# Two attention and mixer layers on one core: VectorE's exponentials in 16-bit fixed point, merged key norms, wider odd units, weights on another queue, and a new order

## The chip, the core and the metric

One core of a Trainium2 chip runs the whole program. Its engines work side by side and meet only through semaphores: TensorE (PE, matmuls from SBUF into PSUM; its weight loads are listed apart as PEld), VectorE (DVE, elementwise work and reductions), ScalarE (ACT, activation functions from tables), GpSimd (POOL) and SyncE (SP, which issues most of the DMAs). PSUM has eight banks of 128x512 fp32 values. The metric is the device time of one execution in microseconds.

## The reference

x is 2048 tokens of 448 values. Two layers, each an attention block and a mixer block with the same weights in both layers:

```python
def _A_ref(x, wqkv, wo):                 # 16 heads of 28
    qkv = (x @ wqkv).reshape(B, S, 3, H, Dh).transpose(2, 0, 3, 1, 4)
    scores = einsum("bhqd,bhkd->bhqk", q, k) * (Dh ** -0.5)
    p = softmax(scores)
    o = einsum("bhqk,bhkd->bhqd", p, v)
    return o.transpose(0, 2, 1, 3).reshape(B, S, D) @ wo
def _B_ref(x, w1, w2, w3, w4):
    h = gelu(layernorm(x) @ w1)
    hs = concat(quarters of h shifted by 1, -1, 2, -2 tokens) @ w2
    x1 = x + hs
    return x1 + gelu(layernorm(x1) @ w3) @ w4
x = x + _A_ref(layernorm(x), A_wqkv, A_wo)
x = x + _B_ref(layernorm(x), B_w1, B_w2, B_w3, B_w4)
# and both once more
```

Most of the elementwise work is the softmax: 2 layers x 16 heads x 2048 x 2048 exponentials, that is 2048 blocks of 128 keys by 512 queries.

## The kernel before

**A planner writes the program.** Every task is a Python generator (t_scores, t_exp, t_pv, k_proj, t_mixA and so on) that yields operations with an estimated duration, waits for named events, and acquires and releases buffers and PSUM banks. A list scheduler (class Sched) plays them through on a model of the engines and writes down, for each engine, the order in which the operations are issued; semaphores follow from reads and writes. Priorities (RANK), leads (Q_LEAD), shares (R_RATE, D_RATE), thresholds and choices of engine (XPAR) are tables of numbers at the top of the file. So a change of a number or of one estimated duration moves the order everywhere. Where the model sees TensorE idle, it inserts filler matmuls (filler, L2165); idle_share is the filler's share of a window, which decisions use.

**Attention.** The work is cut into 68 segments: a layer, a chunk of queries, a group g of four heads, a range of keys. For each segment, blocks of 128x512 scores are computed by TensorE into PSUM banks (L1416). t_scores collects them into units: even units use banks 0, 1, 2 and odd units banks 3, 4. t_exp takes the exponential of a whole unit with one ScalarE instruction (L1654) into the ring PT of 15 slots, and t_pv multiplies by the values into a bank of its own, bank 5 (L825). Queries and keys carry extra rows so that the exponent is shifted by a bound made from key norms; vaug holds the values with a column of ones, which gives the sum.

**VectorE's blocks.** Some blocks are taken out of the stream ahead of time, either in place of the third block of an even unit (R_RATE, bank 2) or as an additional block in a miscellaneous bank (D_RATE, bank 6 or 7), and VectorE computes their exponential. d_first (L1498) writes y = scores x constant as a 32-bit fixed-point number with 16 bits of fraction, and d_chain does the rest: two SCALAR_TENSOR_TENSORs in fp32 evaluate a polynomial in the fraction (L1525, L1527), a TENSOR_SCALAR finishes it into bf16 (L1529), and a last one adds the integer part to the exponent bits (L1532). The estimated durations are in DST. A block is only taken if a buffer for y and a result slot are free, if the planner's recent VectorE load is below XPAR['dt'] (R) or idle_share is at least XPAR['ft'] (D), and as the rates allow.

**Key norms.** For each chunk of keys and each group of heads, k_proj projects (L834), copies the keys out (L1182), squares them (L1168, on GpSimd or VectorE), sums the squares per head with a matmul against astat, and takes the maximum over the keys on VectorE (L1195). t_bias and t_bias4 make the shift from it, which the query projections wait for.

**Other elementwise work.** After each chunk's attention come the output projection and the mixer (t_outproj, t_mixA, t_mixB, t_w4). Their gelu is either a tanh form on ScalarE under the exponential's table, with VectorE and GpSimd doing the rest (tanh_gelu, L1932 to L1935), or a real gelu in a session of its own, with a table load before and after (L2118; L1916 for a chunk that has joined a session).

**Start.** SP issues four tiles of x, then the weights for keys and queries as four DMAs (L860, L862), then wv and the rest of x. ScalarE fills the pads of vaug (L946, L948), packs the weights (t_pack, L963) and squares the first chunks (L975), from which t_ratio makes a scale. t_ln1_first normalises four tiles, TensorE transposes them (L1059), and the first projections follow.

```python
yield op("dve", c_ps(512), lambda e: e.tensor_scalar(out=y, in0=ps[:, bi(bank), :], scalar1=SCALE * L2E * FS, scalar2=-126.0 * FS, op0=ALU.mult, op1=ALU.max),
yield op(D_[0][0], D_[0][1], lambda e: e.scalar_tensor_tensor(out=q, in0=lo, scalar=E2 / E3 * FS, in1=lo, op0=ALU.add, op1=ALU.mult),
```

Of the kernel before, what the change touches and what calls it, by code (L numbers as in the profile page):

```python
# [7 lines left out]
ALU = mybir.AluOpType  # L8
# [176 lines left out]
class Sched:  # L185
# [140 lines left out]
    def keep_pe_busy(self, until):  # L326
# [8 lines left out]
        while True:  # L335
# [21 lines left out]
            if pick is None:  # L357
                if not fits:
                    break
                if self.open5 and all(d.t_end + 0.2 <= t for d in self.P.deps("pe", reads, [key("b5")]).values()):  # L360
                    f_ = self.P.add("pe", lambda e: fn(e, "b5"), reads + [(("xn", 0), "pad")], [key("b5")], t_end=t + dur)
# [188 lines left out]
DST = [('dve', 0.6), ('dve', 0.6), ('dve', 0.34), ('dve', 0.6)]  # L550
DSEG = 1
R_RATE = {(0,): 0, (1,): 0.17, (2,): 0.183, (3,): 0.152, (4,): 0, (5,): 0, (6,): 0.274, (7,): 0.096, (8,): 0.106, (9,): 0.193, (10,): 0.073, (11,): 0.196, (12,): 0.228, (13,): 0, (14,): 0, (15,): 0.457, (16,): 0.306, (17,): 0, (18,): 0, (19,): 0.082, (20,): 0, (21,): 0.089, (22,): 0, (23,): 0.481, (24,): 0, (25,): 0.086, (26,): 0.053, (27,): 0.007, (28,): 0.051, (29,): 0.263, (30,): 0.207, (31,): 0.244, (32,): 0, (33,): 0.012}
# [3 lines left out]
DWIN = 3.0  # L556
# [5 lines left out]
RANK = {('q', 0, 1): 1, ('q', 0, 2): 1.763, ('q', 0, 3): 1.176, ('q', 1, 0): 1.162, ('q', 1, 1): 1.21, ('q', 1, 2): 1.085, ('q', 1, 3): 1.967, ('b', 0, 0): 3, ('b', 0, 1): 2.77, ('b', 0, 2): 1.853, ('b', 0, 3): 2.798, ('b', 0, 4): 1.211, ('b', 1, 0): 2.781, ('b', 1, 1): 1.849, ('b', 1, 2): 2.32, ('b', 1, 3): 2.579, ('b', 1, 4): 2.042, ('a', 0, 0): 1.98, ('a', 0, 1): 1.742, ('a', 0, 2): 1.882, ('a', 0, 3): 1.528, ('a', 0, 4): 2.263, ('a', 1, 0): 2.618, ('a', 1, 1): 1.108, ('a', 1, 2): 1.44, ('a', 1, 3): 1.223, ('a', 1, 4): 1.214, ('k', 0, 1): 2.594, ('k', 0, 2): 2.273, ('k', 0, 3): 2.136, ('k', 1, 0): 2.166, ('k', 1, 1): 1.68, ('k', 1, 2): 1.231, ('k', 1, 3): 2.338, ('k', 1, 4): 2.507, ('c', 0, 0): 1.464, ('c', 0, 1): 1, ('c', 0, 2): 2.866, ('c', 0, 3): 2.39, ('c', 0, 4): 1.764, ('c', 1, 0): 1.835, ('c', 1, 1): 1.44, ('c', 1, 2): 2.171, ('c', 1, 3): 2.127, ('c', 1, 4): 2.53, ('w', 0, 0): 2.816, ('w', 0, 1): 1.099, ('w', 0, 2): 2.277, ('w', 0, 3): 2.222, ('w', 0, 4): 1.537, ('w', 1, 0): 1.87, ('w', 1, 1): 2.531, ('w', 1, 2): 2.03, ('w', 1, 3): 2.877, ('w', 1, 4): 3, ('o', 0, 0): 2.728, ('o', 0, 1): 1.549, ('o', 0, 2): 1.72, ('o', 0, 3): 1.329, ('o', 0, 4): 2.769, ('o', 1, 0): 2.974, ('o', 1, 1): 3, ('o', 1, 2): 1.615, ('o', 1, 3): 1.476, ('o', 1, 4): 1.611, ('v', 0, 1): 1.389, ('v', 0, 2): 2.811, ('v', 0, 3): 3, ('v', 1, 0): 2.33, ('v', 1, 1): 1.844, ('v', 1, 2): 1, ('v', 1, 3): 1.537, ('v', 1, 4): 2.768, ('l', 1, 0): 1.014, ('l', 1, 1): 1.661, ('l', 1, 2): 2.714, ('l', 1, 3): 2.867, ('l', 1, 4): 1.565}  # L562
Q_LEAD = {(0, 1): 14, (0, 2): 51, (0, 3): 92, (1, 0): 95, (1, 1): 20, (1, 2): 92, (1, 3): 88}
D_RATE = {(0,): 0.062, (1,): 0.096, (2,): 0.608, (3,): 0.377, (4,): 0, (5,): 0, (6,): 0.055, (7,): 0.125, (8,): 0.318, (9,): 0.311, (10,): 0.716, (11,): 0.411, (12,): 0, (13,): 0.489, (14,): 0.575, (15,): 0.471, (16,): 0, (17,): 0.052, (18,): 0.128, (19,): 0, (20,): 0.201, (21,): 0.579, (22,): 0.043, (23,): 0.016, (24,): 0.849, (25,): 0.568, (26,): 0.41, (27,): 0.05, (28,): 0.449, (29,): 0, (30,): 0.392, (31,): 0.346, (32,): 0.42, (33,): 0.104}
PE_NORM = {(0, 0): False, (0, 1): False, (0, 2): False, (0, 3): False, (0, 4): False, (0, 5): False, (0, 6): True, (0, 7): True, (1, 0): False, (1, 1): False, (1, 2): False, (1, 3): False, (1, 4): True, (1, 5): True, (1, 6): False, (1, 7): True}
# [9 lines left out]
XPAR = {'l0': 6, 'l1': 11, 'l2': 15, 'x0': 14, ('mg', 0, 0): 0, ('mg', 0, 1): 0, ('mg', 0, 2): 0, ('mg', 0, 3): 1, ('mg', 0, 4): 0, ('mg', 1, 0): 0, ('mg', 1, 1): 1, ('mg', 1, 2): 0, ('mg', 1, 3): 0, ('mg', 1, 4): 1, 'rp': 0.167, 'dp': 3.141, 'dt': 0.642, 'ft': 0.011, ('tw', 0, 0): 0, ('tw', 0, 3): 0, ('tw', 0, 7): 0, ('tw', 0, 11): 1, ('tw', 0, 13): 0, ('tw', 1, 0): 0, ('tw', 1, 3): 0, ('tw', 1, 7): 0, ('tw', 1, 11): 0, ('tw', 1, 13): 0, ('ek', 0, 0): 2, ('eo', 0, 0): 2, ('ek', 0, 1): 0, ('eo', 0, 1): 1, ('ek', 0, 2): 2, ('eo', 0, 2): 2, ('ek', 0, 3): 0, ('eo', 0, 3): 2, ('ek', 0, 4): 0, ('eo', 0, 4): 2, ('eq', 0, 0): 1, ('eq', 0, 1): 1, ('eq', 0, 2): 0, ('eq', 0, 3): 0, ('ez', 0, 0): 2, ('ez', 0, 3): 0, ('ez', 0, 7): 1, ('ez', 0, 11): 2, ('ez', 0, 13): 0, ('ez', 0, 4): 0, ('ez', 0, 8): 0, ('ez', 0, 12): 1, ('ez', 0, 14): 1, ('ex', 0, 0): 2, ('ex', 0, 1): 0, ('ex', 0, 2): 2, ('ex', 0, 3): 2, ('ex', 0, 4): 2, ('ex', 0, 5): 0, ('ex', 0, 6): 2, ('ex', 0, 7): 1, ('ex', 0, 8): 2, ('ex', 0, 9): 1, ('ex', 0, 10): 2, ('ex', 0, 11): 2, ('ex', 0, 12): 0, ('ex', 0, 13): 1, ('ex', 0, 14): 0, ('ex', 0, 15): 2, ('ek', 1, 0): 0, ('eo', 1, 0): 2, ('ek', 1, 1): 1, ('eo', 1, 1): 2, ('ek', 1, 2): 0, ('eo', 1, 2): 1, ('ek', 1, 3): 0, ('eo', 1, 3): 1, ('ek', 1, 4): 1, ('eo', 1, 4): 0, ('eq', 1, 0): 0, ('eq', 1, 1): 0, ('eq', 1, 2): 0, ('eq', 1, 3): 1, ('ez', 1, 0): 1, ('ez', 1, 3): 1, ('ez', 1, 7): 2, ('ez', 1, 11): 2, ('ez', 1, 13): 0, ('ez', 1, 4): 2, ('ez', 1, 8): 2, ('ez', 1, 12): 2, ('ez', 1, 14): 1, ('ex', 1, 0): 2, ('ex', 1, 1): 0, ('ex', 1, 2): 2, ('ex', 1, 3): 0, ('ex', 1, 4): 2, ('ex', 1, 5): 2, ('ex', 1, 6): 1, ('ex', 1, 7): 0, ('ex', 1, 8): 0, ('ex', 1, 9): 0, ('ex', 1, 10): 0, ('ex', 1, 11): 2, ('ex', 1, 12): 0, ('ex', 1, 13): 1, ('ex', 1, 14): 0, ('ex', 1, 15): 0}  # L575
GMERGE = {}
WARM = 0.5
# [22 lines left out]
def build_kernel(nc, A_x, A_wqkv, A_wo, B_x, B_w1, B_w2, B_w3, B_w4, out, n_layers=2):  # L600
# [18 lines left out]
    FS = 65536.0  # L619
    GK = 0.044715  # L620
    E0, E1, E2, E3 = 0.99992525, 0.69583285, 0.22606939, 0.07802301
# [58 lines left out]
    with st:  # L680
# [103 lines left out]
        def op(eng, dur, fn, reads=(), writes=(), **kw):  # L784
            if eng == "pool":
# [1482 lines left out]
```

## Time and profile before

| what | us |
|---|---|
| median of 3 runs | 1028.11 (1027.86 to 1029.22) |
| profiled execution | 1027.56, its span 1025.8 |
| first exponential of the attention starts | 16.20 |
| last one ends | 972.70 |
| 128x1536 exponentials on ScalarE, mean of one | 1.552 (356 of them) |
| 128x1024 exponentials on ScalarE, mean of one | 1.124 (435 of them) |
| VectorE's first step (L1498), to yd / to vaug | 0.687 / 0.684 (85 / 25 of them) |
| gelu sessions' table loads on ScalarE | 1.283 each |

TensorE's granted clock is 1.000 over the span. The views used are: the page (busy time by engine, the chain that ended last); groups of instructions by line, engine and shape, with their count, busy time, the mean of one in ns, and the idle time before them with what ended it; busy time by stretches of the span; and the timeline, which lists an engine's instructions with start and duration. On VectorE and ScalarE the record of an instruction reaches past the start of the next one, so durations do not add up to busy time, and the distance between two starts says what an instruction takes of the engine.

### The profile page before, as it was taken

What the parts mean: (1) busy time and instruction counts of PE and PEld (TensorE: products, weight loads), DVE (VectorE), ACT (ScalarE), POOL (GpSimd) and SP (SyncE); (2) the same over time, 40 slices, a digit from 0 to 9 for tenths busy, and PEclk for the clock granted to TensorE, in tenths of its full rate; (3) what the DMA queues carried; (4) which work ended last, traced back from release to release, by engine and by line L of the source; (5) the groups of instructions that cost most, each with busy time, mean ns of one, the idle gap of its engine ahead of it and who ended that gap; (6) DMA issues with size and microseconds to landing.
All of it is one profiled execution on the core that took longest, in us unless ns stands there. A gap on an engine that the chain in (4) does not pass through costs nothing.

```text
span 1025.8 us, 35791 instructions
## 1 busy us (share of the span) xinstructions
PE 973.6 (95%) x16053; PEld 403.7 (39%) x16053; DVE 830.9 (81%) x1616; ACT 982.3 (96%) x903; POOL 255.0 (25%) x370
## 2 busy tenths in 40 slices
PE   8999999999999999999999999999999999899998
PEld 3333344333343334434334333333334333344465
DVE  7977899989869787878788778898999787787652
ACT  7999999999999999999999999999999999999942
POOL 2124132433134204342233111012313020231120
PEclk9999999999999999999999999999999999999999
DMA  4433453311104003231132015334212111121000
GB/s 121 118 90 103 126 166 89 60 33 38 24 26 98 18 14 100 54 54 24 27 91 77 12 62 161 102 73 120 59 29 38 23 47 41 33 64 36 13 21 24
DMA packets 98808, 64.38 MB, mean 63 GB/s; under 512 B 70816, under 2 KB 87536, under 8 KB 98656
## 3 DMA queue, kind: packets, MB, share of 16 engines
q1 hardware_dynamic: 95280, 54.02, 20.4%
q0 software_dynamic: 3376, 8.09, 2.9%
q8 instruction: 125, 2.05, 0.9%
q14 instruction: 27, 0.22, 0.1%
HBM read 28.16 MB, written 16.76 MB: 44 GB/s over the span
## 4 chain that ended last, share of the span: by engine, by line
ACT 73%; PE 23%; DVE 3%; DMA 0%; issue 0%; SPq 0%; DVEq 0%
ACT PT L1654 65%; PE ps L834 13%; PE ps L1416 5%; PE ps L825 4%; ACT h2T L2118 3%; ACT fb L1934 1%; ACT L1654 1%; PE ps L2165 1%; ACT L2118 1%; DMA PT<-in_A_wqkv_dram 0%; ACT sq L1165 0%; ACT vaug L2118 0%; DVE ub L1738 0%; ACT hT L1916 0%; DVE qT L1217 0%
## 5 line engine op out<-in xcount | busy, mean ns | idle before, releaser
L1654 ACT ACTIVATE PT<-ps 128x1024 bf16<-128x1024 f32 (+1 forms) x791 | 887.0, 1316 | 5.4 <-PE ps L1416 4.1
L1416 PE MATMUL ps<-qT,kT 32*128 32x512 bf16 (+1 forms) x2560 | 309.0, 340 | 27.6 <-ACT PT L1654 19.4
L825 PE MATMUL ps<-PT,vaug 128*32 128x512 bf16 (+1 forms) x2428 | 242.4, 341 | 0.1
L1416 PEld LDWEIGHTS ps<-qT,kT 32*128 32x128 bf16 x2560 | 79.3, 91 | 297.3 <-ACT PT L1654 271.1
L834 PE MATMUL ps<-xT,w 128*32 128x512 bf16 (+4 forms) x2592 | 178.6, 343 | 2.8 <-DVE hT L1903 1.5
L2165 PE MATMUL ps<-ident 128*32 128x256 bf16 x2648 | 121.4, 277 | 1.8 <-POOL ident L919 1.5
L825 PEld LDWEIGHTS ps<-PT,vaug 128*32 128x32 bf16 x2428 | 72.0, 95 | 85.8 <-issue 72.6
L834 PEld LDWEIGHTS ps<-xT,w 128*32 128x32 bf16 (+1 forms) x2592 | 69.9, 95 | 53.8 <-issue 24.6
L834 PE MATMUL ps<-w,h2T 128*32 128x448 bf16 x1288 | 86.2, 355 | 4.1 <-ACT h2T L2118 4.0
L2165 PEld LDWEIGHTS ps<-ident 128*32 128x32 bf16 x2648 | 76.3, 97 | 25.7 <-issue 9.9
L1498 DVE TENSOR_SCALAR yd<-ps 128x512 int32<-128x512 f32 x85 | 58.4, 687 | 20.2 <-PE ps L1416 19.1
L2094 DVE CAST h2T<-ps 128x384 bf16<-128x384 f32 (+1 forms) x84 | 51.9, 618 | 24.4 <-PE ps L834 23.7
L1763 POOL TENSOR_TENSOR otn<-ub,fb 128x512 bf16<-128x512 f32 (+1 forms) x24 | 29.4, 1227 | 127.1 <-DMA fb<-rscr 115.1
L1527 DVE SCALAR_TENSOR_TENSOR fb<-fb,yd 128x512 f32<-128x512 f32 x81 | 60.3, 748 | 0.6
L1525 DVE SCALAR_TENSOR_TENSOR fb<-yd 128x512 f32<-128x512 uint16 x81 | 59.6, 741 | 0.5
L1532 DVE SCALAR_TENSOR_TENSOR PD<-yd,PD 128x512 int16<-128x512 int16 x80 | 56.5, 709 | 1.0
L834 PEld LDWEIGHTS ps<-w,h2T 128*32 128x32 bf16 x1288 | 33.7, 96 | 33.2 <-issue 12.4
L1168 POOL TENSOR_TENSOR sq<-qT 128x512 bf16<-128x512 bf16 x20 | 24.4, 1221 | 85.3 <-DVE qT L1217 85.3
L1168 POOL TENSOR_TENSOR sq<-kT 128x512 bf16<-128x512 bf16 (+2 forms) x24 | 22.9, 955 | 90.6 <-DVE kT L1182 62.4
L834 PE MATMUL ps<-xT,wk_pad 128*32 128x512 bf16 (+1 forms) x512 | 42.8, 369 | 0.1
L834 PE MATMUL ps<-wo_pad,otn 128*32 128x448 bf16 x512 | 38.0, 355 | 2.0 <-DVE x_res L1818 1.6
L2007 POOL TENSOR_SCALAR mst<-mv 128x1 f32<-128x1 f32 x32 | 8.5, 268 | 123.7 <-DVE mv L1021 111.4
(210 smaller groups left out, 1319.7 us busy)
## 6 DMA issues: line engine op xcount, KB each, us to landing
uscr<-ub SPq DMA_DIRECT2D x28, 256.0 KB
ub<-uscr SPq DMA_DIRECT2D x28, 256.0 KB, 3.1
fb<-rscr SPq DMA_DIRECT2D x96, 64.0 KB, 2.0
xnd<-xn SPq DMA_DIRECT2D x28, 128.0 KB, 2.0
x_res<-in_A_x_dram POOLq DMA_DIRECT2D x16, 224.0 KB, 4.3
xd<-x_res SPq DMA_DIRECT2D x16, 224.0 KB, 2.2
x_res<-xd SPq DMA_DIRECT2D x16, 224.0 KB, 2.7
out_dram<-obf SPq DMA_DIRECT2D x16, 112.0 KB, 1.7
```

The costliest lines, as they stand in the source:

```text
L825: return lambda e: e.matmul(out=out, lhsT=lhsT, rhs=rhs, start=start, stop=stop, **kw)
L834: r.append(e.matmul(out=out[c:c + w, :], lhsT=lhsT[:, c:c + w], rhs=rhs, start=start, stop=stop, tile_position=(0, c)))
L1168: return both(kp, 0.15 + NW * 0.0018, 0.07 + NW * 0.00052, lambda e: e.tensor_tensor(out=sq[:, si, 0:NW], in0=src, in1=src, op=ALU.mult), ...
L1416: yield op("pe", (0.005 + NW * 0.00042) / nc_, lambda e, i=i, kc=kc, j=j, g=g, a=a, NW=NW, bank=bank: e.matmul(out=ps[:, bank, i * NW:(i + ...
L1498: yield op("dve", c_ps(512), lambda e: e.tensor_scalar(out=y, in0=ps[:, bi(bank), :], scalar1=SCALE * L2E * FS, scalar2=-126.0 * FS, op0=A ...
L1525: yield op(D_[0][0], D_[0][1], lambda e: e.scalar_tensor_tensor(out=q, in0=lo, scalar=E2 / E3 * FS, in1=lo, op0=ALU.add, op1=ALU.mult), re ...
L1527: yield op(D_[1][0], D_[1][1], lambda e: e.scalar_tensor_tensor(out=q, in0=q, scalar=E1 / E3 * FS * FS, in1=lo, op0=ALU.add, op1=ALU.mult) ...
L1532: yield op(D_[3][0], D_[3][1], lambda e: e.scalar_tensor_tensor(out=pdt.bitcast(I16), in0=hi, scalar=128.0, in1=pdt.bitcast(I16), op0=ALU. ...
L1654: yield op("act", 0.0635 + n * w * 0.000833, lambda e, bk=bk, s0=s0, n=n, w=w: e.activation(out=PT[:, s0:s0 + n, 0:w], in_=ps[:, bk[0]:bk[ ...
L2094: ev = op("dve", c_ps(m * NW), lambda e, hr=hr, pv=pv: e.tensor_copy(out=hr, in_=pv), reads=[("ps", bi(b))], writes=hk, touch=[b])
L2118: yield op("act", c_act(len(fr_) * NW), lambda e, v=v: e.activation(out=v, in_=v, func=ACT.Gelu_apprx_tanh), reads=allk, writes=allk, tab= ...
L2165: return [e.matmul(out=ps[32 * c:32 * c + 32, bi(b), 0:256].rearrange("p (a n) -> p a n", n=128), lhsT=xn[:, 0, D:D + 32] if live else ide ...
```

## The change

- **VectorE's exponential.** FS falls from 65536 to 256: d_first now writes y as int16 with 8 bits of fraction (into the first half of the same buffer). d_chain becomes seven operations on 16-bit data: shift and flip the sign to centre the fraction, a linear term, a square, a scaling, a product, an addition onto y, and a shift that turns the fixed-point number into the bits of a bf16. The result is twice the exponential, so ScalarE's exponentials get a bias of log 2.
- **Key norms.** Except for the first chunk, k_proj ends after the copy. A new task t_knorm squares the four groups of a chunk (into sq and obf buffers), sums them with four matmuls into the four quarters of one bank, and takes one maximum; two small operations and a small matmul distribute it. The bias tasks wait for it.
- **Units.** The PV accumulator moves from bank 5 to bank 7, bank 5 becomes a miscellaneous bank, and an odd unit may take it as third bank when idle_share(8.0) is at least XPAR['wt']. PT's slots are given out in turn (place), and t_exp waits for the blocks that used them before.
- **Start.** The weights for keys and queries are issued by ScalarE's queue as five DMAs (t_wload). Only the pads of vaug's first four slots are filled on ScalarE, the others on GpSimd after the start. Transposes of the first tiles are done tile by tile, and the packing order changes.
- **Order.** All tables of numbers are new; among them XPAR['ft'] from 0.011 to 0.14, XPAR['dt'] from 0.642 to 0.658, and the first layer's chunk 1 joins a gelu session (("mg", 0, 1) from 0 to 1). The sum of the rates times blocks goes from 262 to 217 for R_RATE and from 601 to 582 for D_RATE. Estimated transfer times of the later weights grow. st6 and the bias tables shrink.

```diff
-DST = [('dve', 0.6), ('dve', 0.6), ('dve', 0.34), ('dve', 0.6)]
+DST = [0.2, 0.2, 0.336, 0.2, 0.336, 0.336, 0.2]
...
+PVBANK = 7
...
-    FS = 65536.0
+    FS = 256.0
-    E0, E1, E2, E3 = 0.99992525, 0.69583285, 0.22606939, 0.07802301
+    EA, EB, EG = 21.0427, 88.0467, -0.244205
...
-        MISC = ["b6", "b7", "b5", "b4", "b3", "b2", "b1", "b0"]
+        MISC = ["b6", "b5", "b7", "b4", "b3", "b2", "b1", "b0"]
...
+        def t_wload():
+            for (ci, a, n, t) in ((1, 0, 3, 4.6), (1, 3, 1, 4.3), (0, 0, 1, 4.2), (0, 1, 2, 5.0), (0, 3, 1, 4.6)):
+                src = A_wqkv[128 * a:min(128 * (a + n), D), ci * D:(ci + 1) * D]
+                d3 = wsts[ci]
+                if a == 3:
+                    yield dma("act", lambda e, d3=d3, src=src: e.dma_start(out=d3[0:64, 3, :], in_=src), writes=[("pt", 4 * ci + 3)], t=t, iss=0.55)
...
-            yield op("pool", 0.15, lambda e: e.memset(dcol[:, 0:1], G2 * FS * FS), writes=[("dcol",)])
+            yield op("pool", 0.15, lambda e: e.memset(dcol[:, 0:1], math.log(2.0)), writes=[("dcol",)])
...
+        def t_knorm(L, c):
+            t0, n = KC[L][c]
+            NW = 128 * n
...
+            held = []
+            for g in range(4):
+                yield ("wait", ("k", L, g, c))
...
+                s = yield ("acq", ["ob0", "ob1"] + SQ, dk)
...
+                yield both(("ek", L, c), 0.15 + NW * 0.0018, 0.07 + NW * 0.00052, lambda e, buf=buf, src=src: e.tensor_tensor(out=buf, in0=src, in1=src, op=ALU.mult), dk, [key])
+            b = yield misc(*[h[2] for h in held])
+            yield op("pe", max(0.21, c_mm(NW)), lambda e: [e.matmul(out=ps[32 * g:32 * g + 32, bi(b), 0:NW], lhsT=ind8[:, :], rhs=held[g][1], start=True, stop=True, tile_position=(0, 32 * g)) for g in range(4)],
...
+            yield op("dve", c_ps(NW), lambda e: e.reduce_max(out=kmx[:, :], in_=ps[:, bi(b), 0:NW], axis=AX.X), reads=[("ps", bi(b))], writes=[("kmx",)], touch=[b])
...
+            yield ("sig", ("kn", L, c))
...
-            return (0, 1, 2)[:len(units[u])] if u % 2 == 0 else (3, 4)[:len(units[u])]
+            return (0, 1, 2)[:len(units[u])] if u % 2 == 0 else (3, 4, 5)[:len(units[u])]
...
+            yield op("dve", D_[0], lambda e: e.tensor_scalar(out=qu, in0=yu, scalar1=8, scalar2=32768, op0=ALU.logical_shift_left, op1=ALU.bitwise_xor),
+            yield op("dve", D_[1], lambda e: e.tensor_scalar(out=w, in0=qa, scalar1=EA / 65536.0, scalar2=EB, op0=ALU.mult, op1=ALU.add),
+            yield op("dve", D_[2], lambda e: e.tensor_tensor(out=z, in0=qa, in1=qa, op=ALU.mult),
+            yield op("dve", D_[3], lambda e: e.tensor_scalar(out=z, in0=z, scalar1=1.0 / 65536.0 ** 2, scalar2=EG, op0=ALU.mult, op1=ALU.add),
+            yield op("dve", D_[4], lambda e: e.tensor_tensor(out=z, in0=z, in1=w, op=ALU.mult),
+            yield op("dve", D_[5], lambda e: e.tensor_tensor(out=ya, in0=ya, in1=z, op=ALU.add),
+            yield op("dve", D_[6], lambda e: e.tensor_scalar(out=pdt.bitcast(U16), in0=yu, scalar1=32768, scalar2=1, op0=ALU.bitwise_xor, op1=ALU.logical_shift_right),
...
+                if u % 2 == 1 and SC.idle_share(8.0) >= XPAR['wt']:
+                    gw = yield ("try", [["b5"]])
+                    if gw is not None:
+                        widened.add(u)
+                        lim = 3
...
-                if u >= 6:
-                    for (si, kb, j) in units[u - 6]:
-                        yield ("wait", ("pv", si, kb))
+                for (si, kb) in before[u]:
+                    yield ("wait", ("pv", si, kb))
```

More of the change, by code (lines that the diff above doesn't have):

```diff
@@ L1337, in t_bias4 @@
             yield ("wait", ("rtn",))
[L1338 to L1340 removed]
+            for c in range(p):
+                yield ("wait", ("kn", L, c))
             src, sk = kmaxc[:, L, :, 0], [("kmaxc", L, g, 0) for g in range(4)]
```

216 lines of the change are left out of this document (141 added, 75 removed).

## The prediction

> **What bounds the kernel now.** I read the page's engine totals first, then the three stages, the chain of waits, ScalarE's and VectorE's groups by shape, and last the timeline where VectorE is full.
>
> ```profile
> PE 973.6 (95%) x16053; PEld 403.7 (39%) x16053; DVE 830.9 (81%) x1616; ACT 982.3 (96%) x903; POOL 255.0 (25%) x370
> ...
> ACT 73%; PE 23%; DVE 3%; DMA 0%; issue 0%; SPq 0%; DVEq 0%
> ```
>
> ```profile
> 0.00:16.20 16.20, 12.77 (x239) 7.33 (x243) 11.48 (x51) 11.43 (x17) 5.32 (x18) 1.00 0.67 190
> 16.20:972.70 956.50, 911.01 (x14666) 364.92 (x14666) 799.77 (x1527) 950.61 (x857) 241.73 (x336) 1.00 0.25 63
> 972.70:1025.80 53.10, 49.87 (x1158) 31.44 (x1152) 19.62 (x39) 20.22 (x31) 7.92 (x16) 1.00 0.07 22
> ```
>
> The columns of the second fence are the stretch, its length, then busy time of PE, weight loads, DVE, ACT, POOL. I cut at the first and after the last exponential of the attention. In between, ScalarE is busy 950.6 of 956.5 us: this stage is as long as ScalarE's work. The 16.2 us ahead of it are a chain over all engines, and the 53.1 us behind it belong to TensorE (49.9 busy).
>
> ```profile
> L1654 ACT ACTIVATE PT<-ps 128x1536 bf16<-128x1536 f32 x356 | 552.5, 1552 | 5.0 <-PE ps L1416 4.1
> L1654 ACT ACTIVATE PT<-ps 128x1024 bf16<-128x1024 f32 x435 | 476.0, 1124 | 0.5
> ...
> L1527 DVE SCALAR_TENSOR_TENSOR fb<-fb,yd 128x512 f32<-128x512 f32 x81 | 60.3, 748 | 0.6
> L1525 DVE SCALAR_TENSOR_TENSOR fb<-yd 128x512 f32<-128x512 uint16 x81 | 59.6, 741 | 0.5
> L1498 DVE TENSOR_SCALAR yd<-ps 128x512 int32<-128x512 f32 x85 | 58.4, 687 | 20.2 <-PE ps L1416 19.1
> L1532 DVE SCALAR_TENSOR_TENSOR PD<-yd,PD 128x512 int16<-128x512 int16 x80 | 56.5, 709 | 1.0
> L1529 DVE TENSOR_SCALAR PD<-fb 128x512 bf16<-128x512 f32 x86 | 38.2, 446 | 0.8
> ...
> L1195 DVE TENSOR_REDUCE kmaxc<-ps 128x1 f32<-128x512 f32 x24 | 16.4, 682 | 2.9 <-PE ps L834 2.8
> ...
> L1438 DVE TENSOR_SCALAR qT<-qT,db 128x512 bf16<-128x512 bf16 x28 | 8.3, 348 | 0.1
> ...
> L1168 DVE TENSOR_TENSOR sq<-qT 128x512 bf16<-128x512 bf16 x8 | 3.4, 422 | 0.1
> ```
>
> 356x3 + 435x2 = 1938 of the 2048 score blocks (128x512) go through ScalarE; the other 110 (85 of L1498 above and 25 written to spare vaug slots) go through VectorE. Records overlap, so I price by the distance from one start to the next in the timeline: 1.331 us for three banks, 0.904 for two, hence 0.427 a bank and 0.050 an instruction; a block costs ScalarE (356x1.331 + 435x0.904)/1938 = 0.447 us. The same 791 distances add up to 884 us against 867 at these prices, so a perfect order has about 17 us to find.
>
> ```profile
> 500.60 0.68 DVE L1527 SCALAR_TENSOR_TENSOR fb<-fb,yd 128x512 f32<-128x512 f32 x1
> 501.31 0.43 DVE L1529 TENSOR_SCALAR PD<-fb 128x512 bf16<-128x512 f32 x1
> 501.66 0.61 DVE L1818 TENSOR_TENSOR x_res<-x_res,ps 128x448 f32<-128x448 f32 x1
> ```
>
> L1529 needs L1527's result and starts 0.71 us after it; L1818 needs nothing of L1529 and starts 0.35 after it, before its 0.43 us record has ended. A dependent neighbour costs some 0.11 to 0.12 us more than an independent one; medians are 0.60 against 0.72 for L1525 and L1527.
>
> **VectorE's chain.** Before, per block: 0.608 (L1498) + 2x0.602 + 0.336 + 0.602 = 2.75 us with independent neighbours; the mean distances found are 0.62 + 0.67 + 0.70 + 0.41 + 0.62 = 3.02, so 0.27 goes to dependent neighbours and to waits for GpSimd. After, L1498 stays; four TENSOR_SCALARs and three TENSOR_TENSORs follow, all on 16-bit data in SBUF. For the first the nearest row is L1438, 0.263 start to start with its scalar read from memory; a scalar from memory costs 0.060 (L1217 at 0.668 against L1903 at 0.608, both from PSUM), so 0.203 with an immediate. For the second it is L1168, 0.338. Sum 0.608 + 4x0.203 + 3x0.338 = 2.43 us. The waits: at least the 0.27 of before (2.70, saving 0.32), at most 7/4 of it because seven instructions follow where four did (2.91, saving 0.11). I take 0.20, between the two, as in the full stretches two chains interleave: 110x0.20 = 22 us (12 to 35).
>
> The Trainium skill (VectorE: DVE Perf Modes, Rules for kernel authors) speaks against the change: the pipeline drains after every operation, so the count of operations is to be kept low. It gives about 150 cycles of fixed cost at 0.96 GHz; by that the chain would take an estimated 3.18 us before and 3.12 after. The distances above differ from it: a one-per-cycle operation follows an independent one after 0.60, not 0.69 us.
>
> **No row shows the integer forms** (shift, exclusive or, int16 into bf16). Bounds: 0.203 (L1438's form) and 0.602 (L1532, int16, another form). I take 0.203, the row of the same operation and element size.
>
> **Key norms.** Of 36 maxima (L1195), four of the first chunk stay and 32 become 8. Removed 20x0.60 + 8x0.474 + 4x0.34 = 17.2 us; added 4.3 for eight maxima and 16 small operations at 0.13 (bias rows of L1330 and L1332) = 2.1. VectorE gains 10.8 us, and TensorE 24 groups of four matmuls, some 6 us (16 such take 1.03 in the timeline). The squares stay. The bias operations now wait for all four groups of a chunk; the cover is that they are due segments before their queries, and ScalarE's list of waits names none of them after the first unit. Without it, a late chunk holds ScalarE for about a maximum and two small operations, 0.9 us, eight times at most.
>
> **A gelu joined.** The first layer's second chunk joins an existing gelu session: four tanh at 0.52 become one 1.82, nothing for ScalarE, but eight L1933/L1935 operations of 0.60 leave VectorE: 4.8 us.
>
> **What VectorE's time buys.** 22 + 10.8 + 4.8 = 38 us, at 2.82 a block, is 13 more blocks; 13x0.447 = 5.9 us off ScalarE. From the bounds: 28/2.91 = 10 to 51/2.70 = 19 blocks; none if the planner's new gates refuse them (a bank of TensorE's slack must now be 0.14 idle rather than 0.011, and the summed caps fall from 864 to 799). Low end 0, high end 8.5 us.
>
> **Three-bank odd units.** They need TensorE's filler at 0.166 of the last 8 us. Counting L2165's matmuls over the timeline, 91 of 395 odd units would meet it. Each widened unit carries three blocks and saves 0.4 of an instruction: 91x0.4x0.050 = 1.8 us; they take bank 5 from VectorE's blocks, so 1.0 (0 to 1.8).
>
> **Start.** Before, ScalarE's first packing (L963) starts at 6.63 us, behind two vaug fills of 3.27 us and a 1.24 us wait for weights that SP issued at 2.67. After: five issues on ScalarE's queue, priced by SP's for weights (0.43 to 0.60, so 2.6 us), a table load of 1.28 and a short fill of about 0.5 give 0.79 + 2.6 + 1.28 + 0.5 = 5.2 us. SP is rid of four issues (2.1 us), so wv and the next tiles of x come earlier. Transposes go tile by tile; before, five waited in TensorE's queue from about 8 to 9.27 us behind the sums of squares. VectorE's four statistics, up to 5.85 us, remain. I take 1.8 us off the 16.2 (0 to 2.4). The rest of the vaug pads moves to POOL, two memsets after the start; queued behind them are the key squares, and POOL idles 75%.
>
> **Order.** Priorities, leads and rates are new everywhere. The prize is at most the 17 us above; the loss is in the last 53 us, where TensorE is full and work put off lands at full price (five groups such as those between 1002.9 and 1023.0, 4 us each, are the scale, two of them a bad case: 8 us). I take 2 us of gain.
>
> **Sum.** Against the profiled execution's own 1027.56 us (span 1025.8; the median of the runs is 1028.11, 0.05% above): 1027.6 - 5.9 - 1.0 - 1.8 - 2.0 = 1016.9. **Forecast 1017 us.**
>
> **Rivals.** (1) *The short instructions save nothing* (waits grow with their number): only 15.6 us of VectorE are freed, at 3.02 five blocks, 2.3 us: 1020.5. For it, L1527 to L1529 at 0.71; against it, that two chains do interleave. 0.15. The page's rule cited above leads to this case.
>
> (2) *VectorE takes many more blocks.* Rates are now above zero in nearly every segment, and outside the full stretches named below VectorE is busy 648 of 796 us, 81%. Ten more points over some 700 us is 70/2.82 = 25 blocks, 11 us: 1006. Against it: TensorE is full there. 0.20.
>
> (3) *Slower: an integer form runs at one element a cycle.* In 160 us (116-176, 236-256, 656-696, 736-776) VectorE is busy 151.6, and holds 38 of the 110 blocks. One slow instruction adds 0.40 a block, 15 us there, which nothing hides: blocks land late, the PV matmuls wait, PT slots stay taken and ScalarE stops. The decision is at 10.7/38 = 0.28 us a block, so one slow instruction is enough (1032), and two give 1047. For it: L1532 at 0.602; against it: L1438. 0.08.
>
> (4) *The order gives it back*: banks held by widened units or a tail longer by 8 to 13 us, 1025 to 1030. For it: TensorE at 95%. 0.12.
>
> **How the numbers follow.** Forecast 0.45, rivals 0.15, 0.20, 0.08, 0.12. The forecast and the first two are faster (0.80); of the fourth, half is within 0.2%, about what a measurement can tell from no change here (1026 to 1030), and half is slower or, with the third, 0.14. The range runs from below rival 2's 1006 to the middle of rival 4, 1003 to 1029; the likeliest case alone spans 1010 to 1022.
>
> **What would show it.** The exponential chain's seven instructions behind the first at 0.29 and 0.42 us a record (right) or 0.69 (rival 3); about 123 blocks on VectorE against 110 (rival 2: 140 and more); maxima of keys 12 rather than 36; three-bank instructions on some 90 odd units; the first exponential near 14.4 us; the stage behind the last one still about 53 us. The forecast is wrong if ScalarE shows more than 15 us of waits in the middle stage.

## The result, and the profile after

| | median us (lowest to highest) | ratio to before, 95% interval |
|---|---|---|
| before | 1028.37 (1027.86 to 1029.22) | |
| after | 1093.88 (1091.77 to 1096.46) | 1.0637 [1.0611, 1.0663] |
| forecast | 1017 (1003 to 1029) | |

The change makes the kernel 6.4% slower. Where does the time sit? The page's busy times and its chain of waits for the kernel after:

```profile
PE 998.4 (91%) x16151; PEld 409.5 (37%) x16154; DVE 821.6 (75%) x2012; ACT 1044.3 (95%) x897; POOL 217.1 (20%) x349
...
ACT 89%; PE 8%; DVE 2%; issue 1%; DMA 0%; POOL 0%; SPq 0%; DVEq 0%
```

ScalarE's busy time went from 982.3 to 1044.3 us with six instructions fewer, while VectorE's fell. The three stages, cut as before at the first and after the last exponential (stretch, length, then busy time of PE, weight loads, DVE, ACT, POOL, then the granted clock):

```profile
0.00:18.01 18.01, 13.85 (x210) 7.63 (x211) 12.79 (x50) 8.69 (x16) 7.80 (x20) 0.81 0.59 170
18.01:1043.15 1025.14, 936.72 (x14842) 371.96 (x14843) 789.76 (x1924) 1015.63 (x853) 201.65 (x313) 1.00 0.23 59
1043.15:1094.50 51.35, 47.84 (x1100) 29.91 (x1100) 19.02 (x39) 19.97 (x30) 7.61 (x16) 0.99 0.07 23
```

Of the 68.7 us between the two spans, 68.6 lie in the middle stage, and ScalarE is still busy in all but 9.5 us of it. So it doesn't wait more: its own work has grown. The groups by shape say which:

```profile
L1754 ACT ACTIVATE PT<-ps,sc 128x1536 bf16<-128x1536 f32 x351 | 606.1, 1776 | 5.5 <-PE ps L1487 4.4 <-PE ps L831 1.0
L1754 ACT ACTIVATE PT<-ps,sc 128x1024 bf16<-128x1024 f32 x439 | 546.8, 1341 | 1.9 <-PE ps L1487 1.9
...
L1584 DVE TENSOR_SCALAR yd<-ps 128x512 int16<-128x512 f32 x84 | 57.7, 688 | 34.7 <-PE ps L1487 33.6
L1615 DVE TENSOR_TENSOR fb<-fb 128x512 bf16<-128x512 int16 x96 | 40.9, 431 | 0.6
L1621 DVE TENSOR_TENSOR yd<-yd,fb 128x512 int16<-128x512 int16 x76 | 31.9, 421 | 1.0
L1619 DVE TENSOR_TENSOR fb<-fb,yd 128x512 bf16<-128x512 bf16 x76 | 31.8, 421 | 0.9
L1617 DVE TENSOR_SCALAR fb<-fb 128x512 bf16<-128x512 bf16 x96 | 29.5, 312 | 0.7
```

The exponentials read one thing more: `ps,sc` stands where before had `ps`. sc holds dcol, the log 2 that the change adds as a bias, read from SBUF. A record of 128x1536 grew from 1552 to 1776 ns, one of 128x1024 from 1124 to 1341. By the distance between two starts it is 1.423 against 1.331 us and 0.996 against 0.904: **0.092 us more on each exponential, whatever its width** (medians). 790 x 0.092 = 73 us on the engine that sets the middle stage. VectorE's new steps, in contrast, are as short as forecast (0.29 to 0.43 us a record), its blocks are 117 (110 before), key maxima of 128 x 512 and less are 12 where 36 were, and 28 odd units have a third bank, not 91.

### The profile page after: what moved, and what is told of

It is laid out like the page before. It is cut to its first block, busy times and chain, and to the rows that moved or that the text cites. A ratio compares the mean times of both kernels' runs of the same rounds, so it can differ in the third digit from the quotient of the medians.

```text
span 1094.5 us, 36321 instructions
## 1 busy us (share of the span) xinstructions
PE 998.4 (91%) x16151; PEld 409.5 (37%) x16154; DVE 821.6 (75%) x2012; ACT 1044.3 (95%) x897; POOL 217.1 (20%) x349
## 4 chain that ended last, share of the span: by engine, by line
ACT 89%; PE 8%; DVE 2%; issue 1%; DMA 0%; POOL 0%; SPq 0%; DVEq 0%
ACT PT L1754 82%; PE ps L840 5%; ACT h2T L2220 3%; ACT fb L2036 1%; PE ps L1487 1%; PE ps L831 1%; ACT L1754 1%; PE ps L2267 1%; ACT L2220 0%; ACT hT L2018 0%; DMA h2T<-in_A_x_dram 0%; ACT kT L2220 0%; DVE st L1050 0%; ACT L2018 0%; DVE xn L1070 0%
## 5 line engine op out<-in xcount | busy, mean ns | idle before, releaser
L1754 ACT ACTIVATE PT<-ps,sc 128x1024 bf16<-128x1024 f32 (+1 forms) x790 | 955.5, 1535 | 7.4 <-PE ps L1487 6.3
L1865 POOL TENSOR_TENSOR otn<-ub,fb 128x512 bf16<-128x512 f32 (+1 forms) x31 | 34.8, 1121 | 296.9 <-DMA fb<-rscr 286.3
L840 PE MATMUL ps<-w,h2T 128*32 128x448 bf16 x1288 | 89.6, 355 | 4.0 <-ACT h2T L2220 3.8
L840 PEld LDWEIGHTS ps<-xT,w 128*32 128x32 bf16 (+1 forms) x2592 | 69.2, 95 | 53.7 <-issue 26.6
L2267 PEld LDWEIGHTS ps<-ident 128*32 128x32 bf16 x2620 | 75.8, 98 | 25.3 <-issue 10.1
L1584 DVE TENSOR_SCALAR yd<-ps 128x512 int16<-128x512 f32 x84 | 57.7, 688 | 34.7 <-PE ps L1487 33.6
L840 PE MATMUL ps<-xT,wq_pad 128*32 128x512 bf16 x448 | 40.8, 391 | 0.8 <-DVE kT L1226 0.8
L1615 DVE TENSOR_TENSOR fb<-fb 128x512 bf16<-128x512 int16 x96 | 40.9, 431 | 0.6
L2267 PE MATMUL ps<-ident,xn 128*32 128x256 bf16 x836 | 38.9, 280 | 0.0
L840 PE MATMUL ps<-w,hT 112*32 112x448 bf16 x512 | 36.7, 355 | 1.5 <-ACT hT L2018 1.3
L840 PE MATMUL ps<-wv,xT 128*32 128x448 bf16 x480 | 37.0, 355 | 1.1 <-DVE vaug L1333 0.5
L2105 DVE SCALAR_TENSOR_TENSOR x1b<-x_res,mst,ps 128x448 f32<-128x448 f32 x32 | 21.4, 673 | 21.9 <-PE ps L840 20.6
```

The costliest lines, as they stand in the source:

```text
L840: r.append(e.matmul(out=out[c:c + w, :], lhsT=lhsT[:, c:c + w], rhs=rhs, start=start, stop=stop, tile_position=(0, c)))
L1584: yield op("dve", c_ps(512), lambda e: e.tensor_scalar(out=y.bitcast(I16)[:, 0:512], in0=ps[:, bi(bank), :], scalar1=SCALE * L2E * FS, sca ...
L1615: yield op("dve", D_[2], lambda e: e.tensor_tensor(out=z, in0=qa, in1=qa, op=ALU.mult), reads=fk, writes=fk, urge=urge, two=True)
L1754: yield op("act", 0.0635 + n * w * 0.000833, lambda e, bk=bk, s0=s0, n=n, w=w: e.activation(out=PT[:, s0:s0 + n, 0:w], in_=ps[:, bk[0]:bk[ ...
L1865: yield both(("eo", L, ch), 0.2 + NW * 0.0021, 0.07 + NW * 0.00104, lambda e: e.tensor_tensor(out=otn[:, g, 0:NW], in0=u, in1=rb[:, 0:NW], ...
L2105: yield op("dve", c_ps2(D), lambda e: e.scalar_tensor_tensor(out=X1, in0=X, scalar=mst[:, t, R1:R1 + 1], in1=ps[:, bi(hb), 0:D], op0=ALU.m ...
```

## The experiments

In the tables, "first" is the start of the first exponential, "middle" the length of the middle stage, "waits" the part of it in which no ScalarE record runs, "tail" what follows the last exponential (all of the profiled execution, in us), and "blocks" those on VectorE. Before: first 16.2, middle 956.5, waits 5.9, tail 53.1, blocks 110. The medians are those of all executions, so they can lie some us off the profiled one.

### The bias: as a constant in the new kernel, from SBUF in the old one

a1_imm is the kernel after with one operand changed; the order of every engine stays as it is.

```diff
- func=ACT.Exp, scale=SCALE, bias=dcol[:, 0:1])
+ func=ACT.Exp, scale=SCALE, bias=math.log(2.0))
```

> The changed kernel, every engine's order of instructions kept, with log 2 as a constant in the exponential's instruction instead of a value read from memory (dcol). Theory 1 (the operand in memory costs 0.092 us an instruction): three-bank and two-bank exponentials start 1.331 and 0.904 us apart as before the change, not 1.423 and 0.996; 790 x 0.092 = 73 us are gone and the time is 1021 (1015 to 1027). Rival (the other banks, the 16-bit traffic of VectorE or the new order stretch ScalarE): distances stay at 1.42 and 1.00 and the time stays within 10 us of 1094.

a2_before_ptr is the kernel before, with a zero in dcol read as the exponentials' bias:

```diff
- e.memset(dcol[:, 0:1], G2 * FS * FS)
+ e.memset(dcol[:, 0:1], 0.0)
- func=ACT.Exp, scale=SCALE)
+ func=ACT.Exp, scale=SCALE, bias=dcol[:, 0:1])
```

> The kernel before, in its own order, with a zero read from memory as bias of the exponentials; the values are the same. Theory 1: 791 x 0.092 = 73 us more, 1101 (1095 to 1106), and distances of 1.423 and 0.996. Rival: no change, 1028.

| | median | ratio to before | first | middle | waits | tail | blocks |
|---|---|---|---|---|---|---|---|
| a1_imm | 1029.82 | 1.0016 [1.0007, 1.0025] | 18.08 | 959.1 | 10.4 | 51.3 | 117 |
| a2_before_ptr | 1091.99 | 1.0622 [1.0602, 1.0642] | 16.1 | 1021.2 | 3.0 | 53.1 | 110 |

The groups of ScalarE by shape, a1_imm first:

```profile
L1754 ACT ACTIVATE PT<-ps 128x1536 bf16<-128x1536 f32 x351 | 532.5, 1547 | 6.3 <-PE ps L1487 4.5 <-PE ps L831 1.2
L1754 ACT ACTIVATE PT<-ps 128x1024 bf16<-128x1024 f32 x439 | 467.3, 1118 | 1.6 <-PE ps L1487 1.4
```

and a2_before_ptr:

```profile
L1654 ACT ACTIVATE PT<-ps,sc 128x1536 bf16<-128x1536 f32 x356 | 634.9, 1784 | 2.7 <-PE ps L1416 2.6
L1654 ACT ACTIVATE PT<-ps,sc 128x1024 bf16<-128x1024 f32 x435 | 563.7, 1356 | 0.1
```

The operand takes 64.1 us out of the kernel after and puts 64.6 into the kernel before, less than the 73 expected of both. The distances came out as expected: 1.331 and 0.904 us in a1_imm, 1.423 and 0.997 in a2_before_ptr. The price alone would be 73; the rest is time in which ScalarE would have waited for scores anyway: in a2_before_ptr its waits fall from 5.9 to 3.0, and the distances between exponentials add up to 949 us where the price alone gives 940 (before: 884 where 867 are priced). The Trainium skill (ScalarE: Activation LUTs, What ACT_TABLE_LOAD costs) states it outright: each pointer operand of one value per partition adds about 93 ns to an activation. The traces agree, with 92 from one start to the next.

With the bias out of the way, the other parts together come to +1.6 us by the ratio (0.7 to 2.6 by its interval), against a forecast of -10.7. The runs that follow look for those 12 us.

### The start

> a1 with the first weights issued by SP behind the four tiles of x again; the planner then makes another order. If issuing from ScalarE's queue costs the start (first exponential at 18.0 us after, 16.2 before, with TensorE's granted clock at 0.50 between 9 and 15 us): first exponential at 15 to 16.5 us and a clock of 1.00, the time 2 us below a1, give or take what a new order does. If it is the transposes or the packing order: first exponential stays at about 18.

> a1 with every engine's order kept; the 20th group of filler matmuls at the start is issued ten times over (36 more matmuls, some 1.8 us, up to about 7.4 us). In a1 TensorE stood idle from 5.6 to 7.4 us and its granted clock was 0.50 from 8 to 14 us. If that idle time is what takes the clock away: clock 1.00 throughout, the 16 matmuls of the first key projection take 1.04 us instead of 1.92, the first exponential starts at 16 us instead of 18.1, and the time is 2 us below a1 (1028). Rival (late tiles of x set the start, the clock is a symptom): first exponential within 0.5 us of 18.1.

a3_imm_sp issues the first weights from SP, after the four tiles of x (and so gets an order of its own); a5_imm_warm keeps a1_imm's order and lengthens one group of filler matmuls at the start:

```diff
- for c in range(4)]
+ for _ in range(10 if nfill[0] == 20 else 1) for c in range(4)]
```

| | median | ratio to before | first | middle | waits | tail | blocks |
|---|---|---|---|---|---|---|---|
| a3_imm_sp | 1032.92 (1031.11 to 1040.19) | 1.0066 [1.0043, 1.0089] | 15.46 | 959.4 | 9.9 | 54.1 | 113 |
| a5_imm_warm | 1028.09 | 0.9997 [0.9988, 1.0007] | 15.55 | 958.5 | 10.1 | 51.3 | 117 |

TensorE alone, by stretches of the start (length, busy time, granted clock, DMA share, GB/s), for the kernel after:

```profile
8.00:10.00 2.00, 1.71 (x24) 0.59 1.10 337
10.00:12.00 2.00, 2.00 (x34) 0.50 0.89 269
12.00:14.00 2.00, 2.00 (x28) 0.50 0.03 4
```

and for a5_imm_warm:

```profile
8.00:10.00 2.00, 1.48 (x33) 1.00 1.08 343
10.00:12.00 2.00, 2.00 (x49) 1.00 0.63 199
12.00:14.00 2.00, 1.89 (x33) 1.00 0.02 7
```

The timeline of the kernel after shows what led to it and what it costs:

```profile
3.63 1.92 PE L2267 MATMUL ps<-ident 128*32 128x256 bf16 x40
7.42 0.23 PE L1111 MATMUL ps<-ident,xn 128*128 128x128 bf16 x1 [1.87 <-DVE xn L1065]
...
11.39 1.92 PE L840 MATMUL ps<-xT,wk_pad 128*32 128x512 bf16 x16
```

After its fillers TensorE stands idle for 1.87 us, until the first tile is normalised, and soon after its clock is granted at half. The same sixteen projections that take 1.92 us there take 1.05 in a5_imm_warm. The first exponential is 2.5 us earlier with the clock kept, and 0.65 earlier than before: that is what the new start is worth, and the half clock is most of what turned it into +1.9. Most, not all: the tiles of x do not land at the same time in every execution. The fourth statistics (L1050) start at 6.27 us in the kernel after and at 6.05 in a5_imm_warm, but at 7.08 in a1_imm, where TensorE then stands idle for 3.07 us.

In a3_imm_sp the clock is kept too, and the first exponential comes at 15.46, no later than in a5_imm_warm. So no run shows a gain from the other queue for the weights. Its price shows: the first tile is normalised at 5.97 us in a3_imm_sp and at 5.76 to 5.93 in the nine profiles of the old code's start, but at 6.78 to 8.27 in the eight with the weights on ScalarE's queue, where VectorE waits for the tiles of x to land. That is the gap in which TensorE idles. The time of a3_imm_sp was expected 2 us below a1_imm and is 3.1 above: its order has a tail 2.8 us longer, and four of its ten executions took 1038 to 1040, which the one trace, of the fastest, doesn't explain.

### No third bank for odd units

> a1 without third banks for odd units (28 of them in the changed kernel). Predicted worth 28 x 0.4 x 0.050 = 0.6 us: 1 us slower than a1 or no difference; the rest of a difference is the order's.

```diff
- if u % 2 == 1 and SC.idle_share(8.0) >= XPAR['wt']:
+ if u % 2 == 1 and SC.idle_share(8.0) >= 9.0:
```

1036.81 us, 1.0083 [1.0065, 1.0101]: 7.0 us slower than a1_imm, with 799 units where there were 790. Nine instructions cost 9 x 0.050 = 0.5 us. Between the two profiled executions, 5.2 us apart, ScalarE's waits are 4.8 longer (15.2 for 10.4; two of them, 4.7 us at 743 and 2.8 at 550, have no like in a1_imm) and the tail 2.4 (53.7 for 51.3), while the first exponential comes 1.8 earlier, at 16.25. A part was taken out, and the planner wrote another order; this run can't say how much of the difference is the order's and how much the part's.

### Old and new code under old and new tables

> The kernel before with VectorE's 16-bit chain, its planned durations and the constant log 2 alone; all tables as before. If the chain itself is worth what was forecast (22 us of VectorE, some 8 blocks, 3 us): 1022 to 1030. If a searched order is worth more than the parts and any edit of a part loses it: 1035 or more, although each VectorE block is 0.19 us cheaper.

> a1's code with the tables of before (priorities, rates, leads, choices; the new threshold wt kept at 0.166). Theory 2 (the order is fitted to its code, and the fit is worth 15 us or more): 1035 to 1055. Rival (the parts are worth something in any order): 1030 or less.

> The code of before with the changed kernel's tables. Theory 2: 1040 to 1060, though no instruction is dearer. Rival (the new tables are a better order in themselves): 1027 or less.

b1_chain_only is the kernel before with the 16-bit chain and a constant log 2; b2_new_code_old_tables is a1_imm's code with the tables of before; b3_old_code_new_tables the code of before with the tables of after.

| | median | ratio to before | first | middle | waits | tail | blocks |
|---|---|---|---|---|---|---|---|
| b1_chain_only | 1048.00 | 1.0198 [1.0175, 1.0220] | 16.05 | 972.1 | 21.1 | 62.9 | 110 |
| b2_new_code_old_tables | 1049.65 | 1.0207 [1.0193, 1.0222] | 15.79 | 975.4 | 26.9 | 56.3 | 116 |
| b3_old_code_new_tables | 1059.23 | 1.0304 [1.0287, 1.0321] | 15.85 | 983.2 | 30.3 | 56.9 | 111 |

Every crossing loses 20 to 31 us, and in the middle stage nearly all of it is ScalarE waiting. Each set of tables fits its own code; under the other's it costs more than all parts of the change were forecast to bring. So a part can't be judged by leaving it out or putting it in alone, as a4 and b1 do.

### Both codes under tables that fit neither

The tables were made flat: one value for every priority, one for every rate, all choices of engine alike. One small table, PE_NORM (True for five chunks before and three after), stayed as each code has it, so within a pair not the code alone differs. Flat 0: priorities 2.0, R rates 0.1, D rates 0.25, leads 60. Flat 1: 1.5, 0.15, 0.3, 40. Each ran with the code of before and with a1_imm's.

> The kernel before, its code untouched, with flat tables in place of the sought ones: every priority 2.0, every R rate 0.1, every D rate 0.25, every lead 60, all choices of engine alike, ft 0.08, dt 0.65. Nobody has sought this order, so it serves as the ground on which the two codes are set side by side. 'The parts are worth what was forecast, the order hides it' (T2): this order is some 30 to 80 us worse than before's own, 1060 to 1110 us, and what matters is the distance to its partner c1_flat0_new. 'The parts are worth nothing': the same time here, and the partner within 4 us of it.

> The code of after (16-bit chain, merged key norms, wider odd units, weights on ScalarE's queue) with log 2 as a constant, and the very same flat tables as c1_flat0_old (and 0.166 for the third bank). T2: the parts have a value that a sought order hides, so this is 8 to 20 us faster than c1_flat0_old, with some five more blocks on VectorE and less waiting of ScalarE. 'The parts are worth nothing': within 4 us of c1_flat0_old. 'The parts cost' (wider units and VectorE's seven short steps hold banks longer): slower than it.

> As c1_flat0_old with another set of flat tables (one other set of constants), since one unsought order alone could favour either code by chance. T2: 1060 to 1110 us, to be read only against c1_flat1_new.

> The code of after with a constant log 2 and the flat tables of c1_flat1_old. T2: again 8 to 25 us faster than its partner. If the two pairs differ in sign or by more than 15 us, the worth of the code can't be told apart from the luck of an order, and stays open. 'The parts are worth nothing': within 4 us in both pairs.

> The kernel before with the 16-bit chain and the constant log 2 only, under the flat tables of c1_flat1_old (1091.0) and c1_flat1_new (1073.2), which differ by 17.8 us. If the chain is what the parts are worth, this is near the new code, 1070 to 1080. If the merged key norms, the wider odd units and the start carry it, it is near the old one, 1085 to 1092. An order's luck moves either by some 5 us.

> c1_flat1_new (1073.2) without the third bank for odd units. Forecast by the price of an instruction: 25 widened units, 0.5 us of ScalarE, so 1073 to 1075. In a sought order their removal cost 7 us (a4_imm_nowide against a1_imm), which by the price of an instruction can't be. If it costs 5 us and more here too, a third bank is worth more than ScalarE's instructions, for it lets units of three go on where VectorE's blocks hold bank 2; if less, the 7 us were the order's.

| | median (lowest to highest) | first | middle | waits | tail | blocks |
|---|---|---|---|---|---|---|
| c1_flat0_old | 1089.40 (1087.78 to 1095.70) | 15.60 | 994.9 | 49.7 | 75.5 | 125 |
| c1_flat0_new | 1080.84 (1071.48 to 1082.00) | 16.45 | 979.9 | 37.8 | 82.6 | 131 |
| c1_flat1_old | 1090.99 (1090.28 to 1091.56) | 15.78 | 1011.2 | 65.7 | 62.1 | 125 |
| c1_flat1_new | 1073.19 (1072.34 to 1075.07) | 18.14 | 990.5 | 47.5 | 64.3 | 134 |
| d2_flat1_chain | 1064.94 (1064.39 to 1065.01) | 15.66 | 981.3 | 36.2 | 66.1 | 127 |
| d3_flat1_new_nowide | 1079.38 (1077.79 to 1083.34) | 17.08 | 992.8 | 50.4 | 67.4 | 136 |

The new code is 8.6 us faster in the first pair and 17.8 in the second; the sign holds in both. (Of c1_flat0_new's four values three are near 1081 and one is 1071.5; the profiled one has a granted clock of 0.93 in its tail.) Six blocks more (131 for 125) are worth 6 x 0.447 = 2.7 us of the first middle's 15.0, and nine are 4.0 of the second's 20.7; most of the rest are waits that fell by 11.9 and 18.2. The chain alone (d2, with the PE_NORM of before) gains 26.1 us with two blocks more, and its waits fall by 29.5; it lies below both ranges that I had given it. Without third banks (d3) the new code loses 6.2, where its 25 widened units are worth 0.5 by the price of an instruction. By the sign set for that run, 5 us and more, a third bank is worth more than the instructions that it saves, as a4_imm_nowide's 7.0 had it; but 3.3 of the 6.2 are one wait, of 15.0 us for 11.7 at some 580 us, so the order's chance isn't ruled out.

ScalarE's waits in c1_flat1_old (what waited, for what: us in total, times, longest),

```profile
ACT PT L1654 <- PE ps L1416: 27.5, 17, 14.8
ACT fct L1361 <- DVE dbc L1375: 18.0, 1, 18.0
```

and in d2_flat1_chain:

```profile
ACT PT L1660 <- PE ps L1416: 23.6, 12, 14.2
...
ACT fct L1361 <- DVE dbc L1375: 8.0, 1, 8.0
```

These orders have single waits of 8 to 18 us that no sought order has; 10.0 of d2's 26.1 us come out of one of them. So the pairs show, as far as PE_NORM allows, that the code has a value under such orders, and that it lies in work that reaches ScalarE sooner more than in blocks taken from it. Its size in a well-sought order they don't give. That the chain alone beats all parts together here by 8.3 us may be the order's chance, for the gains of the two pairs lie 9.2 us apart; no run shows it.

### The chain under before's own order

> The kernel before with the 16-bit chain in place of its four steps and log 2 as a constant, and with before's order of every engine kept instruction for instruction: the seven new steps stand in the places of the four old ones (two, two, two, one), and the planner is given the old durations. It has no other part of the change and no more blocks on VectorE. Theory 'the chain is worth its busy time only where more blocks are taken': VectorE's busy time falls by about 20 us (110 x 0.19), ScalarE's work stays 884 us, and the time falls by no more than the 5.9 us that ScalarE waits in the middle: 1023 to 1028, ratio 0.995 to 1.000. Rival 'the chain itself costs' (b1_chain_only was 20 us slower): seven dependent steps end later and hold buffers, so this too is slower than before, 1035 to 1048. If it is not slower, the 20 us of b1_chain_only are the new order's and not the chain's.

> As d1_chain_same_order (before's order, 16-bit chain, constant log 2, no more blocks), but of the 330 second halves of the paired steps 241 are moved behind the next instruction on VectorE that doesn't need them; nothing else is moved. In d1 all 330 followed the step that they need at once, and the chain took 3.15 us of VectorE a block, more than before's 3.02, though the same steps take 2.84 in a1_imm, where 240 of 700 neighbours depend on each other. Theory 'dependent neighbours made d1 slow': the chain falls to 2.8 to 2.95, VectorE has 8 to 25 us less to do than before, and the time falls from 1034 to 1021 to 1028, at or below the kernel before. Rival 'any departure from the order that before was sought for costs 5 us and more, whatever VectorE has to do': 1030 to 1036 again. Second rival, latency: a block's chain takes longer from its first to its last step when steps stand apart (8.5 us in the median before and in d1), and if it grows past 9.5 us, the values matmuls wait and the time stays above 1030.

Both keep the order in which before issues its work. In d1 the seven steps stand in the four old places, two to a place; d4 moves 241 of the 330 second halves behind the next instruction that doesn't need them.

```diff
- e.scalar_tensor_tensor(out=q, in0=lo, ...)
+ Seq([lambda e: e.tensor_scalar(out=qu, in0=yu, ...),
+      lambda e: e.tensor_scalar(out=w, in0=qa, ...)])
```

| | median | ratio to before | middle | waits | chain, us a block | stretched steps, extra us |
|---|---|---|---|---|---|---|
| before | | | 956.5 | 5.9 | 3.02 | 22, 15.3 |
| d1_chain_same_order | 1033.95 | 1.0068 [1.0054, 1.0082] | 962.0 | 10.0 | 3.15 | 33, 24.9 |
| d4_chain_spread | 1033.91 | 1.0063 [1.0049, 1.0077] | 963.1 | 10.5 | 3.06 | 32, 23.2 |
| a1_imm | 1029.82 | 1.0016 [1.0007, 1.0025] | 959.1 | 10.4 | 2.84 | 23, 13.8 |

Both miss what I expected: d1 lies between its two ranges, and d4 in the range of its rival, by which any departure from the sought order costs 5 us and more. Its second rival, latency, is out: from its first step to its last a block takes 8.6 us in the median of d4 and 8.5 in d1 and before, not over 9.5. "Chain" is the sum of the mean distances from each step's start to the next instruction's, over the steps behind which VectorE doesn't stand idle. In d1 a first step that its successor needs holds VectorE for 0.356 us on average (0.321 in the median), where an independent neighbour follows after 0.202 in a1_imm; with 330 such pairs the new chain is dearer than the old one. d4 mends less than a third of that: in the new places many steps again stand beside one that they need (336 of 660 steps have the chain's next step right behind them, where d1 has 430).

A second suspect stands in the last column: steps of the chain whose record is over 0.2 us longer than the median of their line. In every one of those steps, in all four kernels, a GpSimd instruction runs at the same time. VectorE in d4:

```profile
284.80 1.17 DVE L1575 TENSOR_TENSOR fb<-fb,yd 128x512 bf16<-128x512 bf16 x1
285.88 0.55 DVE L2141 CAST h2T<-ps 128x384 bf16<-128x384 f32 x1
286.35 1.47 DVE L1576 TENSOR_TENSOR yd<-yd,fb 128x512 int16<-128x512 int16 x1
```

and GpSimd in the same stretch:

```profile
284.64 1.04 POOL L1979 TENSOR_TENSOR fb<-hT 112x512 f32<-112x512 bf16 x1 [9.12 <-DVE hT L1950]
286.27 1.27 POOL L1810 TENSOR_TENSOR otn<-ub,fb 128x512 bf16<-128x512 f32 x1 [0.59 <-DMA fb<-rscr]
```

Two steps of 0.43 us take 1.17 and 1.47: each starts just after a GpSimd instruction and ends some 0.3 after it. Just behind this place, at some 290 us, the exponentials lose 0.9 us to before, and 1.0 more at 760 to 762, behind two more such steps at 754 and 757. In d1 and d4 together an exponential falls back against before by over 0.3 us at 17 places; 14 of them lie within 7 us behind the start of a stretched step, though such stretches are only a fifth of the middle stage. They hold 4.1 of the 5.5 us by which d1's middle is longer, and 3.1 of d4's 6.6. The Trainium skill (SBUF — State Buffer, Who interferes with whom) says that VectorE and GpSimd share a pair of ports under an exclusive lock, and that the order of issue decides who is blocked; the rows agree. The old order had been sought with the old steps in it, and the new ones meet GpSimd 10 or 11 times more, for 8 to 10 us. So the places speak for GpSimd rather than the dependent neighbours; no run tests it by itself, with GpSimd's work moved out of the way.

## Why the prediction was wrong

**The step that failed is one that the sum doesn't contain:** the bias of log 2. My account of the change names it, and the prediction then costs 110 blocks, key norms, a gelu, units, start and order, but not the operand on 790 instructions of the engine that it had just found to bound the kernel. Costed at nothing, it measured 64 us, five sixths of the 77 between 1017 and 1094. I had the price of the like operand on VectorE in my own sum (0.060, from L1217 against L1903) and used it there to take it off a step. No rival held it either; rival 3, the slower one, was about the wrong engine. Nor could the sign set for a wrong forecast catch it: more than 15 us of waits on ScalarE were to show, and the kernel after has 9.5, because the missing term is work and not a wait.

**Right, by the runs:** ScalarE bounds the middle stage, so whatever changes its work shows at nearly full price. The chain's saving: forecast 0.20 us a block, 0.19 measured in a1_imm (3.02 to 2.84) and 0.16 after. The 16-bit integer forms run at 0.202 in the median (the four TENSOR_SCALARs, three of them on integers, beside an independent neighbour), so rival 3 is out. Rival 1, that short instructions save nothing, is out in these two orders, and with it the rule that led to it (the Trainium skill, VectorE: DVE Perf Modes, Rules for kernel authors); in d1, where steps that need each other stand side by side, the new chain did cost 3.15 for 3.02. Key maxima fell from 36 to 12, and four tanh on ScalarE and eight operations on VectorE left with the joined gelu, as counted.

**Sizes that were off, all read in a1_imm, without the bias:**

- *Blocks.* 13 more were forecast, 7 came: -3.1 us for -5.9. VectorE is busy 16 us less (814.8), so time was free; something refused the blocks, as the "low end 0" allowed for. That it was the gates isn't shown.
- *Odd units.* 28 widened, not 91: I counted them in before's order. By the instruction, 0.6 us; but the two runs without them lost 7.0 and 6.2, so the price may be the wrong one, and their worth stays open.
- *Start.* -1.8 became +1.9, most of it by the clock. I had compared queues and durations but not asked whether TensorE would stand idle longer. With the clock kept it is -0.65. Of the 1.15 still missing, 1.0 lies ahead of the first normalised tile, which starts at 6.78 in a5_imm_warm where it started at 5.76: VectorE waits 0.25 and 0.66 us there for the first two tiles of x to land, and before it waited for neither. I counted on wv and the next tiles of x to come earlier, and not on the first ones to land later with the weights issued beside them.
- *Order.* +2 us of gain was forecast; ScalarE's waits in the middle rose by 4.5 (5.9 to 10.4), which eats the blocks' gain, and the tail gave 1.8 back. By its time this remainder is rival 4's (1025 to 1030), but not by its mechanism: the tail is shorter, not longer, and without the widened units the kernel is slower, not faster. What I didn't see is how much of a part's worth an order decides: 20 to 31 us in b1 to b3.

**Why faster VectorE work brought so little** is partly open. Shown: before's order leaves 5.9 us of waits in the middle, so beyond these freed VectorE time can only pay through more blocks, and 7 came; under flat orders, with 50 and 66 us of waits, the same code saves 9 and 18 us. Not shown: what the parts are worth in an order sought for them as long as before's was. No run beats the kernel before; a5_imm_warm equals it.

## What to carry to other kernels

Go through the operands of the bounding engine's most frequent instruction before anything else: here a scalar read from SBUF instead of a constant cost 0.09 us each time, and 790 times that outweighed every other part of this change by far. When the order of a kernel was sought for its code, compare codes under neutral orders, more than one of them, or after a search for each, for a part taken out of a sought order is charged with the order's loss. And when work at the start is moved, ask what TensorE does in the new gap.

## What was unexpected of the hardware

- One per-partition operand in SBUF adds 0.092 us to an activation's start-to-start distance at both widths (1.331 to 1.423, 0.904 to 0.996), and 0.22 to 0.23 to its record.
- After 1.87 us of an idle TensorE, from 5.55 to 7.42, its clock was granted at 0.50 from about 8 to about 15 us, though it was busy again from 7.42 on; ten times as many matmuls in one filler group, which leave 0.55 us of idle time there, kept it at 1.00. Idle times of 1.53 to 3.07 us at this place also came before a half clock in a1_imm, a4_imm_nowide, c1_flat0_new and d3_flat1_new_nowide, and 1.36 us in b2_new_code_old_tables did not. In c1_flat1_new, after 2.71 us, the clock is listed at 1.00, though the sixteen projections take 1.75 us.
- A short 16-bit VectorE step can take three times its duration beside GpSimd (0.43 to 1.17 and 1.47 us), and a dependent neighbour adds 0.11 to 0.13 us in the median, more than half of what a step of 0.202 takes by itself.
